# Where a second product stands between first products: moving TensorE's work to the last step of each batch

## The chip, the cores and the metric

The kernel runs on one core of a Trainium2 chip. The metric is the device time of one execution in microseconds. The core has five engines with a queue each: TensorE (PE, matrix products), VectorE (DVE), ScalarE (ACT), GpSimd (POOL) and SyncE (SP, which issues the transfers). TensorE writes its products into eight PSUM banks of 128 x 512 float32, from which ScalarE and VectorE read them.

## The reference, cut to what matters

```python
def _attn_ref(x, state):                 # x (4, 8, 512, 64), state (4, 8, 32, 64)
    a = softmax(scale * x @ state.T)     # xread = a @ state
    a2 = softmax(scale * state @ x.T)    # sread = a2 @ x
    return concat([xread, sread])        # 4 batches of 512 + 32 tokens, 512 wide

def _moe_ref(x, w_in, w_out):            # w_in (512, 2048), w_out (2048, 512)
    h = x @ w_in
    g = np.maximum(h, 0.0) + np.log1p(np.exp(-np.abs(h)))
    return (g @ w_out)

def _moe2_ref(x, w_gate, w_val, w_out):  # 512 -> 1536 -> 512
    g = x @ w_gate
    silu = g * (1.0 / (1.0 + np.exp(-g)))
    return (silu * (x @ w_val) @ w_out)
```

The three run one after the other: attention, then the layer with the softplus, then the layer with the gate.

## The kernel before

Every float32 operand of the two layers is split in two float32r parts, a high one (a copy, on ScalarE, which rounds) and a low one (whole minus high, `low`, L77, on VectorE or GpSimd). A product is then three matmuls, high x high, low x high and high x low (`mm3`, L71 to 74), each of 128 x 128 by 128 x 512.

**Prologue.** It loads tokens and states, does the softmaxes and the states' reads, and makes the first weights. **Stage 1** is the layer with the softplus, the loop of L800 to L825. **Stage 2**, the loop of L880 to L932, is the gated layer.

Stage 1 works on units (c, b, ft): chunk c of four takes 512 of the 2048 hidden columns, b is one of four batches of 512 tokens, and ft one of four tiles of 128 hidden columns. There are 64 units and 64 steps n. A unit is a first product `p1` (L419; six matmuls into a bank `ph`), a softplus on ScalarE twice (`h` rounded and `C` whole, L411 and L414), a subtraction on GpSimd (`l`, `g_low`, L433) and a second product `p2` (L442; twelve matmuls into four banks `py`, one for each 128 output columns, which collect over the four ft of a batch). After ft 3 the four `py` are added to the sums `yacc` by VectorE (`y_add`, L451; in the first chunk L456 copies, in the others L458 adds), two at the start of the step's VectorE work and two later. The second products of the next batch start in the same four banks, so they wait for these. In step n TensorE does `p2` of unit n, then what hangs on the step, then `p1` of unit n + LAG, with LAG = 4 (L806 to L808); ScalarE and GpSimd then make `h`, `C` and `l` of unit n + 3.

What hangs on a step is put there by `at(step, kind, function)`: "pe" runs between `p2` and `p1`; "dve0" at the start of VectorE's work of the step (ahead of the first `y_add`), "dve1" at its end; "act" and "pool" likewise. On TensorE three things hang there in every chunk but the last, for the chunk that comes next: eight products `pm` of three matmuls (`m_mm`, L369), which give the tokens' factors `m` from the weights `win` (copied by ScalarE, L396, and subtracted by VectorE, `m_low`, one step later); and the state tokens' own layer, `s1` (L507; twelve matmuls into `ps`), a softplus, `s2` (four transposes into `ptgs`), a copy and a subtraction for the result `gs`, `s3` (L532; twelve matmuls into `ps`) and `s4` (L540; VectorE, the sum into `ys`, L545). VectorE also prepares weights (`t_win`, `t_wo`, `t_gv`, `t_w`; L122 to L140), for the next chunk and, in the last chunks, for stage 2, and in the last chunk sums of `yacc` that stage 2 reads (`y_sums`, L474 to L480, results `T`).

TensorE's, VectorE's and SyncE's orders are as the code writes them. ScalarE's and GpSimd's are set by a scheduler. An allocator gives each product a PSUM bank: four tags, 4 banks for "y", 3 for "h" (`ph`) and 1 for "m" (`pm`, `ps`, `ptgs`), share eight banks, and which product gets which bank, and so for whose eviction it has to wait, changes with the order. In chunk c, steps count from 16 c.

Of the kernel before, what the change touches and what calls it, by code (L numbers as in the profile page):

```python
# [22 lines left out]
def attention_moe_moe2_kernel(  # L23
# [44 lines left out]
    def bank(tag, name):  # L68
        return psum.tile([P, 512], F32, tag=tag, bufs=BUFS[tag], name=name)

    def mm3(o, a, b, first, last, **k):  # L71

        for i, (s, t) in enumerate(((0, 0), (1, 0), (0, 1))):
            nc.tensor.matmul(o, a[s], b[t], start=first and i == 0, stop=last and i == 2, **k)  # L74
# [344 lines left out]
    def p1(u):  # L419
        c, b, ft = u  # L420
        ps = bank("h", f"ph{c}_{b}_{ft}")
        f = slice(ft * P, (ft + 1) * P)
        for hg in range(NHG):
            mm3(
                ps, [mt[c, b, hg][:, i, f] for i in range(2)], [aT[b, hg][:, i, :] for i in range(2)],
                hg == 0, hg == NHG - 1,
            )
        n = f"{c}_{b}_{ft}"
        sp[u] = Softplus(
            ps, work.tile([P, 512], F32, tag="C", name=f"C{n}"), work.tile([P, 512], F32R, tag="GH", name=f"h{n}")  # L430
        )

    def g_low(u):  # L433
        l = work.tile([P, 512], F32R, tag="GL", name="l%d_%d_%d" % u)
        low(nc.gpsimd, l, sp[u].g, sp[u].h)
        gT[u] = (sp[u].h, l)
# [5 lines left out]
    def p2(u):  # L442
        c, b, ft = u
        if ft == 0:
            for dt in range(KT):
                yps[dt] = bank("y", f"py{c}_{b}_{dt}")
        t = gT.pop(u)
        for dt in range(KT):
            mm3(yps[dt], [wo[c, ft].out[:, i, dt * P:(dt + 1) * P] for i in range(2)], t, ft == 0, ft == FT - 1)

    def y_add(c, b, dt):  # L451
        if c == 0 and dt % 2 == 0:
            yacc[b, dt // 2] = slot([P, 2, 512], F32, "yacc", f"yacc{b}_{dt // 2}")
        v = yacc[b, dt // 2][:, dt % 2, :]
        if c == 0:
            nc.vector.tensor_copy(v, yps[dt])  # L456
        else:
            nc.vector.tensor_tensor(out=v, in0=yps[dt], in1=v, op=ALU.add)  # L458
# [118 lines left out]
    act = {}  # L577
# [79 lines left out]
    LAG = 4  # L657
    M_STEPS = (6, 7, 9, 10, 14, 15, 17, 18)
    with tc.manual_schedule(engines={ENG.PE}):
        units = [(c, b, ft) for c in range(NCK) for b in range(B) for ft in range(FT)]  # L660
        NU = len(units)
# [45 lines left out]
        def at(n, kind, fn, *args):  # L707
            hooks.setdefault((n, kind), []).append((fn, args))

        def run(n, kind):  # L710
            for fn, args in hooks.get((n, kind), ()):
                fn(*args)

        def at_weights(n, late, store, key, make):

            def begin():
                store[key] = make(*key)
            at(max(0, n - 4), "load", begin)
            for m, kind, step in (
                (n, "dve0", "head"), (n, "act", "square"), (n + late, "dve1", "tail"),  # L720
                (n + late + 1, "act", "high"), (n + late + 1, "pool", "low"),
            ):
                at(m, kind, lambda step=step: getattr(store[key], step)())

        for c in range(NCK):
            n0 = c * UC
            if c + 1 < NCK:
                pieces = [(win, piece_win, (c + 1, k)) for k in range(KT)] + [(wo, piece_wo, (c + 1, k)) for k in range(FT)]
            else:
                pieces = []  # L730
            for i, (store, make, key) in enumerate(pieces):
                n, late = n0 + i // 2 * FT + i % 2, 2 - 2 * (i % 2)
                at_weights(n, late, store, key, make)
            if c + 1 < NCK:
                for i in range(2 * KT):
                    n = n0 + M_STEPS[i]
                    k = (c + 1, i // KT, i % KT ^ 1)
                    at(n, "pe", m_mm, *k)
                    at(n, "act", m_high, *k)
                    at(n + 1, "dve0", m_low, *k)  # L740
            if c + 1 < NCK:
                for i, kind, fn in (
                    (10, "pe", s1), (11, "act", s1_first), (16, "pe", s2), (16, "act", s2_high), (17, "dve0", s2_low),
                    (20, "pe", s3), (21, "dve0", s4),
                ):
                    at(n0 + i, kind, fn, c + 1)
        for k in range(1, KT):
# [52 lines left out]
        with tc.manual_schedule(engines={ENG.DVE, ENG.SP}):  # L800
            for n in range(1 - LAG, NU):
                run(n, "load")
                if n >= 0:
                    u = units[n]
                    p2(u)
                    run(n, "pe")  # L806
                    if n + LAG < NU:
                        p1(units[n + LAG])  # L808
                nx = units[n + LAG - 1] if n + LAG - 1 < NU else None
                if nx:  # L810
                    sp[nx].high()
                    sp[nx].whole()
                last = n >= 0 and u[2] == FT - 1
                run(n, "dve0")
                for dt in range(2) if last else ():
                    y_add(u[0], u[1], dt)
                run(n, "act")
                if nx:
                    g_low(nx)
                run(n, "pool")  # L820
                for dt in range(2, KT) if last else ():
                    y_add(u[0], u[1], dt)
                run(n, "dve1")
                run(n, "act1")
                run(n, "pool1")  # L825
            for n in range(NU, NU + FT + 1):
                for kind in ("act", "dve0", "pool"):
                    run(n, kind)
# [11 lines left out]
        for k, j in enumerate(range(len(EARLY), 3 * NF)):  # L840
            n, half = divmod(k, 2)
# [134 lines left out]
```

## Time and profile before

| what | us |
|---|---|
| median of 3 runs | 788.11 (787.13 to 790.48) |
| the profiled execution | 788.33 |
| its span | 786.4 |
| TensorE busy | 743.8 (95%) |
| VectorE busy | 511.2 (65%) |
| ScalarE busy | 354.1 (45%) |
| GpSimd busy | 418.7 (53%) |

What ends last is followed back through TensorE for 69% of the span, and through VectorE for 15%. The shares are an average over stages: stage 1 has the waits, stage 2 hardly any. Matmuls overlap at their ends, so 389 ns of busy time for one go with starts 227 ns apart.

### The profile page before, as it was taken

How to read it: one execution, taken by the hardware profiler on the slowest of the kernel's cores; microseconds unless marked ns; L12 is line 12 of the kernel's file. 1: busy time of each engine (PE TensorE's matmuls, PEld its weight loads, DVE VectorE, ACT ScalarE, POOL GpSimd, SP SyncE). 2: the span in 40 equal slices, each digit the busy share in tenths (PEclk: the TensorE clock that was granted, in tenths of full speed). 3: DMA queues.
4: the chain of work that ended last, by engine and by line, in shares of the span. 5: the costliest groups of instructions: out<-in, count | busy, mean ns of one | idle time of the engine just before them, and what ended most of it. 6: DMA issues, size and time to landing. Idle time of an engine off the chain costs nothing.

```text
span 786.4 us, 9643 instructions
## 1 busy us (share of the span) xinstructions
PE 743.8 (95%) x3280; PEld 600.9 (76%) x3280; DVE 511.2 (65%) x725; ACT 354.1 (45%) x643; POOL 418.7 (53%) x371
## 2 busy tenths in 40 slices
PE   6586999999999999899899999999999999999997
PEld 3345787888788888777678888888888888888886
DVE  5899586686887688779668767575563343343334
ACT  5576465464656555654354444433253223322320
POOL 3578465547565747688467667655355213212311
PEclk9688999999999999999899999999999999999999
DMA  9712132424343424455739798978437737436412
GB/s 340 298 57 80 54 135 82 133 81 145 109 142 114 162 79 152 143 193 200 276 126 349 271 379 313 314 276 325 161 119 273 230 141 248 155 133 231 158 40 108
DMA packets 51217, 144.03 MB, mean 183 GB/s; under 512 B 5728, under 2 KB 18016, under 8 KB 51168
## 3 DMA queue, kind: packets, MB, share of 16 engines
q1 hardware_dynamic: 51168, 143.42, 52.3%
q8 instruction: 26, 0.43, 0.2%
q14 instruction: 23, 0.19, 0.1%
HBM read 107.48 MB, written 35.91 MB: 182 GB/s over the span
## 4 chain that ended last, share of the span: by engine, by line
PE 69%; DVE 15%; DMA 6%; issue 4%; POOL 4%; ACT 2%; SPq 1%; DVEq 0%; ACTq 0%; POOLq 0%
PE py L74 18%; PE po L74 15%; PE px L74 14%; PE pz L74 7%; PE ph L74 6%; PE pt L74 3%; DMA gw<-gv_d 2%; DMA raw_gv<-in_moe_w_val_dram 2%; PE ps L74 2%; PE pm L74 2%; DVE m L77 1%; POOL l L77 1%; DVE t_wo L136 1%; DVE yacc L458 1%; DVE t_gv L126 1%
## 5 line engine op out<-in xcount | busy, mean ns | idle before, releaser
L74 PE MATMUL py<-h,wo 128*128 128x512 f32 x512 | 162.7, 400 | 9.8 <-DVE yacc L458 8.0
L74 PE MATMUL po<-w,h 128*128 128x512 f32 x384 | 126.2, 391 | 0.0
L74 PEld LDWEIGHTS py<-h,wo 128*128 128x128 f32 x512 | 98.3, 193 | 32.4 <-DVE yacc L458 9.8
L77 POOL TENSOR_TENSOR l<-C,h 128x512 fp32r<-128x512 f32 x64 | 90.5, 1416 | 44.9 <-ACT C L414 40.6
L77 POOL TENSOR_TENSOR l<-cA,h 128x512 fp32r<-128x512 f32 x24 | 35.2, 1465 | 143.9 <-ACT h L582 143.9
L74 PE MATMUL py<-l,wo 128*128 128x512 f32 x256 | 102.1, 399 | 5.0 <-POOL l L77 5.0
L74 PE MATMUL ph<-aT,m 128*128 128x512 f32 x384 | 97.8, 391 | 1.4 <-DVE m L77 1.1
L603 DVE TENSOR_TENSOR oacc<-po,oacc 128x512 f32<-128x512 f32 x80 | 54.7, 690 | 56.5 <-PE po L74 56.2
L74 PEld LDWEIGHTS ph<-aT,m 128*128 128x128 f32 x384 | 71.9, 188 | 16.8 <-issue 1.3
L74 PEld LDWEIGHTS po<-w,h 128*128 128x128 f32 x384 | 72.1, 188 | 14.8
L74 PE MATMUL po<-w,l 128*128 128x512 f32 x192 | 74.8, 390 | 0.5 <-POOL l L77 0.5
L77 DVE TENSOR_TENSOR m<-pm,m 64x512 fp32r<-64x512 f32 (+1 forms) x60 | 41.2, 687 | 45.3 <-ACT m L396 41.2
L74 PE MATMUL px<-T_0s,gw 128*128 128x512 f32 x216 | 61.3, 392 | 1.8 <-ACT cC L907 1.7
L74 PEld LDWEIGHTS py<-l,wo 128*128 128x128 f32 x256 | 49.4, 193 | 16.1 <-POOL l L77 5.4
L74 PE MATMUL px<-T_1s,gw 128*128 128x512 f32 x216 | 60.7, 389 | 0.0
L191 POOL TENSOR_TENSOR sums_gv<-t_gv 128x128 f32<-128x128 f32 x48 | 23.0, 500 | 53.2 <-DVE t_gv L140 49.8
L896 DVE TENSOR_TENSOR cA<-py,cA 128x512 f32<-128x512 f32 x24 | 16.5, 689 | 50.2 <-PE py L74 46.9
L74 PEld LDWEIGHTS px<-T_0s,gw 128*128 128x128 f32 x216 | 40.1, 188 | 11.6 <-ACT cC L907 2.6
L582 ACT ACTIVATE h<-cA 128x512 fp32r<-128x512 f32 x24 | 15.2, 632 | 71.6 <-DVE cA L915 71.6
L74 PEld LDWEIGHTS px<-T_1s,gw 128*128 128x128 f32 x216 | 40.5, 188 | 8.5
L74 PEld LDWEIGHTS po<-w,l 128*128 128x128 f32 x192 | 36.1, 188 | 8.3 <-POOL l L77 1.0
L77 POOL TENSOR_TENSOR l<-cC,h 128x512 fp32r<-128x512 f32 x24 | 31.8, 1326 | 18.8 <-ACT h L582 17.3
(159 smaller groups left out, 1517.5 us busy)
## 6 DMA issues: line engine op xcount, KB each, us to landing
gw<-gv_d SPq DMA_DIRECT2D x96, 512.0 KB, 6.6
gv_d<-gv SPq DMA_DIRECT2D x24, 512.0 KB, 3.3
gv_d<-split_gv SPq DMA_DIRECT2D x24, 512.0 KB, 4.0
w<-w_d SPq DMA_DIRECT2D x24, 512.0 KB, 8.8
raw_win<-in_moe_w_in_dram SPq DMA_DIRECT2D x16, 512.0 KB, 4.6
raw_wo<-in_moe_w_out_dram SPq DMA_DIRECT2D x16, 512.0 KB, 3.8
raw_gv<-in_moe_w_gate_dram SPq DMA_DIRECT2D x48, 128.0 KB, 3.3
raw_gv<-in_moe_w_val_dram SPq DMA_DIRECT2D x48, 128.0 KB, 2.8
```

What stands on the lines that cost most here:

```text
L74: nc.tensor.matmul(o, a[s], b[t], start=first and i == 0, stop=last and i == 2, **k)
L77: eng.tensor_tensor(out=o, in0=whole, in1=high.bitcast(F32), op=ALU.subtract)
L126: nc.vector.scalar_tensor_tensor(out=ti, in0=self.top, scalar=-0x40000000, in1=ti, op0=ALU.bitwise_and, op1=ALU.bitwise_or,)
L136: nc.vector.scalar_tensor_tensor(out=ti, in0=self.bot, scalar=29, in1=ti, op0=ALU.logical_shift_right, op1=ALU.bitwise_or,)
L191: nc.gpsimd.tensor_tensor(out=o, in0=x, in1=y, op=op)
L458: nc.vector.tensor_tensor(out=v, in0=yps[dt], in1=v, op=ALU.add)
L582: nc.scalar.activation(h, src, AF.Copy)
L603: nc.vector.tensor_tensor(out=v, in0=ps, in1=v, op=ALU.add)
L896: nc.vector.tensor_tensor(out=c["A"], in0=y, in1=c["A"], op=ALU.add)
```

## The change

Two edits. In the loop, `p1` is no longer called once a step for unit n + 4: in the steps of ft 0 and 1 it still is, in that of ft 2 none is called, and in that of ft 3 two are, for units n + 3 and n + 4. In the table, three steps of the state tokens move: `s1` from the third step of a batch (10) to the fourth (11), `s3` from the first step of a batch (20) to the last of the one ahead of it (19), and `s4` from VectorE's start of step 21 to its end of step 20.

```diff
                 for i, kind, fn in (
-                    (10, "pe", s1), (11, "act", s1_first), (16, "pe", s2), (16, "act", s2_high), (17, "dve0", s2_low),
-                    (20, "pe", s3), (21, "dve0", s4),
+                    (11, "pe", s1), (11, "act", s1_first), (16, "pe", s2), (16, "act", s2_high), (17, "dve0", s2_low),
+                    (19, "pe", s3), (20, "dve1", s4),
                 ):
...
                     p2(u)
                     run(n, "pe")
-                    if n + LAG < NU:
-                        p1(units[n + LAG])
+
+
+                    for k in ((n,), (n,), (), (n - 1, n))[u[2]]:
+                        if k + LAG < NU:
+                            p1(units[k + LAG])
```

In the changed file, lines below the loop are three further down. VectorE's queue has the same order as before from the start of stage 1 on. The other engines' orders follow here at three places; names carry the batch and the tile (the chunk is left out), then a number.

TensorE at the boundary of steps 51 and 52 in the last chunk, before: the end of the first step of batch 1, whose `py` are done before `ps` (`s3`).

```order
L74 MATMUL ph_1_3_3007<-aT_1_250,m_1_1_2557 128x512 x3
L74 MATMUL py_1_0_3046<-h_1_0_2877,wo_0_2653 128x512 x2
...
L74 MATMUL py_1_3_3049<-l_1_0_2936,wo_0_2653 128x512
L74 MATMUL ps_3062<-wo_0_2653,gs_2885 128x512 x3
L74 MATMUL ps_3062<-wo_1_2614,gs_2885 128x512 x3
L74 MATMUL ps_3062<-wo_2_2827,gs_2885 128x512 x3
L74 MATMUL ps_3062<-wo_3_2782,gs_2885 128x512 x3
L74 MATMUL ph_2_0_3075<-aT_0_305,m_2_0_2784 128x512 x3
```

And now, from the last `py` of batch 0 on:

```order
L74 MATMUL py_0_3_2851<-l_0_3_2892,wo_3_2773 128x512
L74 MATMUL ps_2998<-wo_0_2653,gs_2885 128x512 x3
L74 MATMUL ps_2998<-wo_1_2591,gs_2885 128x512 x3
L74 MATMUL ps_2998<-wo_2_2827,gs_2885 128x512 x3
L74 MATMUL ps_2998<-wo_3_2773,gs_2885 128x512 x3
L74 MATMUL ph_1_2_3011<-aT_0_201,m_1_0_2422 128x512 x3
L74 MATMUL ph_1_2_3011<-aT_1_250,m_1_1_2557 128x512 x3
L74 MATMUL ph_1_3_3020<-aT_0_201,m_1_0_2422 128x512 x3
L74 MATMUL ph_1_3_3020<-aT_1_250,m_1_1_2557 128x512 x3
L74 MATMUL py_1_0_3059<-h_1_0_2877,wo_0_2653 128x512 x2
```

Between the last `py` of batch 0 and the first of batch 1 stood six matmuls (one `ph`); now 24 stand there (`ps` and two `ph`). In the other batches it is twelve.

ScalarE in the second chunk around steps 21 to 23, before (`m` is the copy of a `pm` into the two batches' factors, `split_gv` that of sums which GpSimd makes):

```order
L411 ACTIVATE h_2_1_1666<-ph_2_1_1658 128x512
L414 ACTIVATE C_2_1_1665<-ph_2_1_1658 128x512
L396 ACTIVATE m_0_0_1713<-pm_0_1_1693 64x512
L396 ACTIVATE m_1_0_1715<-pm_0_1_1693 64x512
L195 ACTIVATE split_gv_1_1809<-sums_gv_1_1767 128x512
L411 ACTIVATE h_2_2_1705<-ph_2_2_1697 128x512
```

And now:

```order
L411 ACTIVATE h_2_1_1667<-ph_2_1_1659 128x512
L414 ACTIVATE C_2_1_1666<-ph_2_1_1659 128x512
L195 ACTIVATE split_gv_1_1809<-sums_gv_1_1767 128x512
L396 ACTIVATE m_0_0_1704<-pm_0_1_1693 64x512
L396 ACTIVATE m_1_0_1706<-pm_0_1_1693 64x512
L396 ACTIVATE m_0_0_1704<-pm_0_0_1728 64x512
L396 ACTIVATE m_1_0_1706<-pm_0_0_1728 64x512
L411 ACTIVATE h_2_2_1740<-ph_2_2_1732 128x512
```

The copy of `pm_0_1` stood ahead of `split_gv` and now stands behind it. In the banks, `ph_2_2` here is in the bank that `pm_0_1` had; before, the two had different ones. Other such pairs in the changed program, each a product in the bank of the one named behind it: in step 7 `ph` of batch 2, ft 2 and the `pm` of the same step; in step 11 `ps` and the `ptgs` of step 10; in step 47 `ph` of batch 0, ft 2 and the `pm` of step 46.

GpSimd in the last chunk, from the sums of batch 0 to the first `l` of batch 3, before:

```order
L77 TENSOR_TENSOR l_2_2_3214<-C_2_2_3152,h_2_2_3153 128x512
L191 TENSOR_TENSOR sums_gv_1_3220<-t_gv_1_3156,sums_gv_1_3220 128x128
L77 TENSOR_TENSOR B_0_0s<-yacc_1_1031,B_0_0s 128x512
L77 TENSOR_TENSOR l_2_3_3267<-C_2_3_3197,h_2_3_3198 128x512
L77 TENSOR_TENSOR split_gv_1_3260<-sums_gv_1_3220,split_gv_1_3260 128x512
L77 TENSOR_TENSOR B_0_1s<-yacc_1_1031,B_0_1s 128x512
L77 TENSOR_TENSOR l_3_0_3298<-C_3_0_3250,h_3_0_3251 128x512
L77 TENSOR_TENSOR w_3374<-t_w_3254,w_3374 128x512
```

And now:

```order
L77 TENSOR_TENSOR l_2_1_3156<-C_2_1_3118,h_2_1_3119 128x512
L77 TENSOR_TENSOR B_0_0s<-yacc_1_1031,B_0_0s 128x512
L77 TENSOR_TENSOR l_2_2_3214<-C_2_2_3188,h_2_2_3189 128x512
L77 TENSOR_TENSOR split_gv_1_3260<-sums_gv_1_3220,split_gv_1_3260 128x512
L77 TENSOR_TENSOR B_0_1s<-yacc_1_1031,B_0_1s 128x512
L77 TENSOR_TENSOR l_2_3_3267<-C_2_3_3197,h_2_3_3198 128x512
L77 TENSOR_TENSOR w_3374<-t_w_3254,w_3374 128x512
L77 TENSOR_TENSOR l_3_0_3298<-C_3_0_3250,h_3_0_3251 128x512
```

Each `l` has moved behind work for stage 2 that stood after it.

## Rows read from the trace of the kernel before

**Rows 1.** Windows, stages 1 and 2: busy us (instructions) by engine, clock, DMA share, GB/s.

```profile
67.00:391.00 324.00, 306.95 (x1327) 251.06 (x1326) 249.36 (x323) 170.60 (x305) 201.43 (x176) 0.97 0.41 137
391.00:786.40 395.40, 388.65 (x1778) 322.06 (x1776) 207.43 (x294) 139.93 (x242) 177.85 (x160) 1.00 0.61 216
```

**Rows 2.** Waits of TensorE: total us, times, longest us.

```profile
PE py L74 <- DVE yacc L458: 8.0, 2, 5.3
PE py L74 <- POOL l L77: 5.0, 1, 5.0
```

**Rows 3.** Timeline of TensorE: start us, us, operation, count, [idle before and its releaser].

```profile
132.78 1.62 PE L74 MATMUL ph<-aT,m 128*128 128x512 f32 x6 [1.12 <-DVE m L77]
211.07 2.74 PE L74 MATMUL ps<-win,sT 128*128 128x512 f32 x11 [1.13 <-DVE m L77]
334.94 1.22 PE L74 MATMUL py<-h,wo 128*128 128x512 f32 x2 [2.68 <-DVE yacc L458]
363.79 0.62 PE L74 MATMUL py<-h,wo 128*128 128x512 f32 x2
367.87 0.62 PE L74 MATMUL py<-h,wo 128*128 128x512 f32 x2
377.42 1.22 PE L74 MATMUL py<-h,wo 128*128 128x512 f32 x2 [5.31 <-DVE yacc L458]
```

**Rows 4.** Windows over three second products and over VectorE's stretch without a wait.

```profile
343.29:346.17 2.88, 2.88 (x14) 2.41 (x13) 2.78 (x5) 1.91 (x4) 0.21 (x1) 1.00 0.94 349
334.94:339.37 4.43, 4.43 (x13) 3.59 (x14) 2.90 (x5) 4.34 (x8) 4.43 (x6) 0.65 0.42 169
377.42:382.73 5.31, 5.31 (x14) 4.15 (x15) 2.89 (x4) 3.56 (x8) 4.73 (x5) 0.53 1.00 334
...
342.12:376.69 34.57, 29.99 (x132) 24.32 (x130) 34.12 (x35) 15.62 (x28) 27.07 (x23) 0.98 0.63 215
```

**Rows 5.** Timeline of VectorE, as rows 3.

```profile
114.57 1.38 DVE L77 TENSOR_TENSOR m<-pm,m 64x512 fp32r<-64x512 f32 x2
194.90 1.39 DVE L77 TENSOR_TENSOR m<-pm,m 64x512 fp32r<-64x512 f32 x2 [2.89 <-ACT m L396]
334.19 2.49 DVE L458 TENSOR_TENSOR yacc<-py,yacc 128x512 f32<-128x512 f32 x4
337.05 0.83 DVE L126 SCALAR_TENSOR_TENSOR t_w<-raw_w,t_w 128x512 int32<-128x512 int32 x1
342.12 0.69 DVE L545 TENSOR_TENSOR ys<-ps,ys 128x512 f32<-128x512 f32 x1 [4.25 <-PE ps L74]
343.80 0.68 DVE L77 TENSOR_TENSOR B_0s<-yacc,B_0s 128x512 fp32r<-128x512 f32 x1
364.84 1.78 DVE L476 TENSOR_TENSOR yacc<-yacc,yacc 128x512 f32<-128x512 f32 x1
376.69 2.47 DVE L458 TENSOR_TENSOR yacc<-py,yacc 128x512 f32<-128x512 f32 x4
```

**Rows 6.** Waits of VectorE over the span, as rows 2.

```profile
DVE ys L545 <- PE ps L74: 9.8, 3, 4.3
```

**Rows 7.** Timeline of GpSimd, as rows 3.

```profile
340.24 1.29 POOL L77 TENSOR_TENSOR l<-C,h 128x512 fp32r<-128x512 f32 x1
345.96 1.45 POOL L191 TENSOR_TENSOR sums_gv<-t_gv 128x128 f32<-128x128 f32 x2 [3.18 <-DVE t_gv L140]
364.33 1.75 POOL L77 TENSOR_TENSOR l<-C,h 128x512 fp32r<-128x512 f32 x1
368.42 1.29 POOL L77 TENSOR_TENSOR B_1s<-yacc,B_1s 128x512 fp32r<-128x512 f32 x1 [0.64 <-ACT B_1s L490]
374.62 1.59 POOL L77 TENSOR_TENSOR w<-t_w,w 128x512 fp32r<-128x512 f32 x1 [3.22 <-ACT w L146]
```

**Rows 8.** Timeline of ScalarE, as rows 3.

```profile
193.67 1.20 ACT L396 ACTIVATE m<-pm 64x512 fp32r<-64x512 f32 x2
197.37 0.63 ACT L195 ACTIVATE split_gv<-sums_gv 128x512 fp32r<-128x512 f32 x1 [2.50 <-POOL sums_gv L191]
```

## The prediction

> **What bounds the kernel now.** I read the windows by stage first, then the waits of TensorE, then the moments of those waits, then VectorE and GpSimd in the last chunk. Stage 2 (391 to 786.4 us) is bound by TensorE: busy 388.65 of 395.40 us at granted clock 1.00 [rows 1]. Nothing in it is edited and its instructions on VectorE keep their order, so I carry it unchanged; whatever stage 1 ends earlier or later, the program does. Stage 1 holds TensorE busy for 306.95 of 324.00 us [rows 1], so 17 us is all that any reordering could win, plus what the clock costs. The waits name most of it: 8.0 us for `y_add` on VectorE in two waits and 5.0 once for the first `l` [rows 2]. The two are at 334.94 (2.68 us) and 377.42 (5.31 us); two smaller ones, 1.12 at 132.78 and 1.13 at 211.07, are for an `m` of VectorE whose bank a `ph` and a `ps` take over [rows 3]. Behind the two long ones TensorE starts at its lower clock level: granted 0.65 over the second product that follows at 334.94 and 0.53 over that at 377.42, against 1.00 over one that follows no wait, at 343.29 [rows 4]. Twelve matmuls and their tail take 2.88 us there, 4.43 at 0.65 and 5.31 at 0.53, so the clock adds 1.55 and 2.43 us to the waits of 2.68 and 5.31.
>
> The two long waits have different causes. At 334.94 VectorE is in time with its queue, and the six matmuls of one `ph` between the two batches (1.36 us at the pace of 0.227 us a matmul, which is 2.72 us for the twelve of a second product; 363.79 to 367.87 is one of each [rows 3]) are too short a cover for the four `y_add` (2.49 us from 334.19 [rows 5]). At 377.42 VectorE itself is late. It waits 4.25 us for `ps`, starts `ys` at 342.12 [rows 5], and has hardly a gap from there on: 34.12 us busy in the 34.57 us up to the `y_add` of 376.69 [rows 4]. So this last boundary is set by when VectorE begins at 342.12 and how fast it then works. Its speed hangs on GpSimd. An operation of two SBUF inputs takes 1.78 us at 364.84 beside a GpSimd operation of 1.75 us at 364.33, while one of the same size takes 0.68 us at 343.80, where GpSimd pauses until 345.96; GpSimd's `l` takes 1.29 us at 340.24, in the stretch where VectorE waits [rows 5, 7]. While both run, one of each takes about 1.75 us, against 0.68 + 1.29 = 1.97 one after the other: running together saves 11%, no more.
>
> **The change, part by part.** No instruction is added or removed in the stage, so at full clock TensorE's own work is unchanged; SyncE's transfers change neither number nor size, and VectorE's queue keeps its order through the stage (the end of step 20 is the place ahead of the start of step 21, so `s4` passes nothing there). What moves is TensorE's order, and with it the scheduler's orders of ScalarE and GpSimd and the PSUM banks.
>
> (1) *Two `ph` and, once a chunk, `s3` between two batches.* Two `ph` take 12 x 0.227 = 2.72 us, with `s3` 5.44, against 1.36. At 334.94 the cover grows by 4.08 us and the loss there is 2.68 + 1.55 = 4.23, so that stall nearly goes; it is the largest sure gain on TensorE. By itself it does not enter the sum: VectorE sets the next boundary, and what TensorE gains here it waits for at 377.42. At the other boundaries there was no wait to win.
>
> (2) *VectorE no longer waits for `ps`.* Without a lag `s3` now ends at 332.1, some 10 us earlier: the `ph` of steps 50 and 51, the `py` of step 52 and the lost 4.23 us no longer stand before it. VectorE was free at 337.88, so `ys` could start up to 4.25 us earlier; waits of the same sort in two chunks before make the sum 9.8 us over three [rows 6], off the critical path. But in those 4.25 us GpSimd ran alone at 1.29 us [rows 7]; now both run together. By the 11% above, 4.25 us of GpSimd and some 4 us of VectorE that now run together are worth 0.11 x 8.3 = 0.9 us, against 4.25 if VectorE kept its pace of 0.69. I take 0.5, since the lag of TensorE, below, delays the `y_add` of that boundary as well. The Trainium skill (SBUF — State Buffer, Who interferes with whom) says that a VectorE instruction with two SBUF inputs contends with a GpSimd instruction that reads SBUF, and that the one that comes second is blocked until the first has finished. The rows above go the same way (1.78 beside 1.75), though some 1.75 for a pair is less than the sum of both; by the strict rule the earlier start would be worth 0 instead of 0.5.
>
> (3) *New owners of PSUM banks.* The allocator now gives some `ph` the bank of an `m` product that is evicted later. In step 7 `ph` of batch 2, ft 2 takes the bank of the `pm` of that step, whose `m` subtraction stands in VectorE's queue behind the `y_add` and runs at 114.57 to 115.95 [rows 5]; TensorE would be there at 113.4, so it waits 2.6 us. In step 11 `ps` takes the bank of the transposed tokens, which are copied (0.6) and subtracted (0.69) only behind what stands ahead of them: some 2, estimated, with the 1.12 of step 10 gone. Step 23 is the dearest: `ph` takes the bank of the `pm` of step 22, whose `m` was copied by ScalarE at 193.67 and subtracted by VectorE at 194.90; in ScalarE's new order that copy stands behind `split_gv`, which waited until 197.37 for GpSimd's sums [rows 5, 8]. Copy 1.2 and subtraction 1.4 after that give 200.6, two `ph` 203.3, and the next second product started at 197.54: 5.8 later, with the `y_add` of that step queued behind. Step 47 repeats it with nothing to wait for from GpSimd: some 1.6, the two subtractions of an `m` and what is queued before them. The bounds of all four are 0 (if the sums come earlier) and their sum, 12. Against them go 1.13 of 211.07 [rows 3] and some quarter microseconds. I carry a lag of TensorE of +3 after step 12, +6 after 24 and +5.5 at step 48. It is paid out of the stall that (1) removes (4.23) and out of the 5.31 us of waiting at 377.42: TensorE had that much to spare.
>
> (4) *Later `l` in the last chunk.* GpSimd's new order puts every `l` behind one or two more operations: that of the last step of batch 2 ran at 364.33, 1.8 us before its second product at 367.87; it now stands behind B_1s (368.42) and would end near 371.4, a wait of some 3 us on TensorE [rows 3, 7]. This too lies inside the wait that ended at 377.42. The `l` of the first step of the last batch now stands behind `w` (374.62 and 1.59 long [rows 7]), so it ends near 377.9: +0.6 on the path.
>
> (5) *The clock at the last boundary.* By (3) and (4) TensorE reaches the last boundary late and in pieces, so that its idle stretch there is some 1 to 2 us instead of 5.31. After the wait of 1.12 us six matmuls took 1.62 us [rows 3], 0.1 over six starts and a tail at full clock. Then the 2.43 us of 377.42 are won. Bounds: 0 and 2.43; I take 2.43.
>
> (6) *The prologue* has another order on ScalarE and GpSimd; the first `l` stands behind two more subtractions of 1.29 us, which would make the 5.0 us wait [rows 2] longer by up to 2.6, while what those subtractions delayed before comes earlier: -1.5 to +1.5, taken as 0.
>
> Sum against the profiled execution: 788.33 - 0.5 (2) - 2.43 (5) + 0.6 (4) = 786.0. The median of the runs is 788.11, 0.2 below that execution, so I leave 786.0.
>
> **The rivals.** *The gain is kept in full* (0.25): the sums of step 22 come in time, the lag is under 3 us, VectorE starts `ys` 4.25 us earlier and works off its short operations before GpSimd takes the port; then the last `y_add` is 3 to 4.25 us earlier and the clock gains 2.43: 788.3 - 4.25 - 2.43 = 781.6, or 783 with part of it. For it: in 342 to 346 VectorE did have GpSimd's pause. Against: it now has GpSimd's three operations there.
> *Slower* (0.17): the bank waits of (3) and GpSimd's order of (4) are not absorbed. It decides when TensorE's lag at step 48 passes what `ys` can spare: `s3` would end at 332.1 plus the lag, and VectorE is free at 337.88, so from a lag of 5.8 on VectorE starts later by the rest, and from 5.8 + 4.25 = 10 on it starts later than now. With all four waits at their price (12) and nothing won back before step 48 but 2.3, the lag is near 10, and late `l` on GpSimd add 3 + 2.6 that then are on the path: +4 to +8, about 793.
> *Nothing moves* (0.13): VectorE and GpSimd in sum set the last boundary, TensorE waits long enough there to lose its clock as now, and the gain at 334.94 is only waited for later: 788 to 789.
> *The forecast* (0.45) lies at 784.5 to 787.5.
>
> **How the numbers follow.** Half a per cent is 3.9 us, about what a measurement of this kernel can tell from no change. Faster by more: the full gain, 0.25, and the lower end of the forecast, 0.04. Slower by more: 0.17. Within: the rest, 0.54. The range goes from the full gain (781.5) to the near end of the slower case (792): it leaves out the very best tail and about two thirds of the slower one.
>
> **What would show it.** Right: no wait at the boundary of steps 51 and 52; no wait of VectorE for `ps`; clock 1.00 in the first second product of the last batch; new waits of `ph` for `m` in steps 7 and 23, of 2 to 6 us each; operations of VectorE at 1.7 us where `ys` now stands; stage 2 at 395 us. Wrong: clock 0.5 in the last batch (then 788 or more), the last `y_add` more than 2 us earlier (then 783), TensorE over 10 us late at step 48, or a stage 2 that differs by more than 1 us.

## The result and the profile after

The changed kernel takes 799.78 us (median of 4 runs, 798.28 to 801.45) against 788.33 (4 runs, 787.13 to 790.48): a ratio of 1.0143, interval 1.0113 to 1.0173. It is slower by three times what a measurement can tell, and above the whole range. The profiled execution took 799.57 us, so 13.6 us stand between it and the forecast.

The page gives the busy times, and a window the second stage (busy us and instructions of TensorE, its weight loads, VectorE, ScalarE and GpSimd; then TensorE's clock, DMA share, GB/s).

```profile
span 797.8 us, 9665 instructions
PE 745.7 (93%) x3280; PEld 603.2 (76%) x3280; DVE 509.0 (64%) x725; ACT 354.7 (44%) x643; POOL 417.3 (52%) x371
```

```profile
401.40:797.80 396.40, 388.74 (x1777) 323.27 (x1775) 203.97 (x294) 140.43 (x242) 176.37 (x160) 1.00 0.62 217
```

All engines do the work they did before. Stage 2 begins at 401.4 and not at 391.3 and takes 396.4 us instead of 395.1 (the row of [rows 1] begins a little earlier, at 391.00): ten of the eleven microseconds are lost in stage 1. There the two waits for `y_add` of [rows 2] have gone from the list of TensorE's waits, and these stand in it (total us, times, longest):

```profile
PE ph L74 <- DVE m L77: 7.2, 3, 5.1
PE py L74 <- POOL l L77: 4.0, 2, 2.0
...
PE px L74 <- ACT cC L910: 3.1, 2, 2.4
...
PE ps L74 <- DVE yacc L456: 2.4, 1, 2.4
...
PE ps L74 <- DVE gs L77: 1.8, 1, 1.8
```

TensorE's timeline has the moment of each (start, us, operation, count, idle time before and its releaser):

```profile
113.91 4.62 PE L74 MATMUL ps<-win,sT 128*128 128x512 f32 x12 [2.41 <-DVE yacc L456]
...
138.55 3.06 PE L74 MATMUL ps<-win,sT 128*128 128x512 f32 x12 [1.81 <-DVE gs L77]
...
206.31 4.81 PE L74 MATMUL ph<-aT,m 128*128 128x512 f32 x12 [5.12 <-DVE m L77]
...
286.47 3.00 PE L74 MATMUL ph<-aT,m 128*128 128x512 f32 x12 [1.22 <-DVE m L77]
...
325.72 2.96 PE L74 MATMUL ph<-aT,m 128*128 128x512 f32 x12 [0.89 <-DVE m L77]
...
362.90 0.50 PE L74 MATMUL py<-l,wo 128*128 128x512 f32 x1 [2.01 <-POOL l L77]
...
383.16 0.50 PE L74 MATMUL py<-l,wo 128*128 128x512 f32 x1 [2.00 <-POOL l L77]
...
389.91 0.61 PE L74 MATMUL py<-h,wo 128*128 128x512 f32 x2
...
424.11 0.96 PE L74 MATMUL px<-T_0s,gw 128*128 128x512 f32 x3 [2.44 <-ACT cC L910]
```

The first five are products whose PSUM bank another product still holds. Two of them cost more than the wait itself. Windows over the twelve matmuls behind these two show it; the third window is the first second product of the last batch, which follows no wait:

```profile
113.91:118.53 4.62, 4.62 (x13) 3.65 (x14) 4.47 (x7) 1.96 (x4) 2.26 (x2) 0.63 0.03 7
206.31:211.12 4.81, 4.81 (x13) 3.87 (x14) 4.73 (x9) 1.64 (x3) 0.65 (x1) 0.60 0.01 3
389.91:392.80 2.89, 2.89 (x15) 2.37 (x14) 0.95 (x2) 1.54 (x4) 2.89 (x3) 1.00 1.01 339
```

At a granted clock of 0.63 and 0.60 twelve matmuls take 4.62 and 4.81 us, against 2.88 at 1.00 [rows 4]: 1.74 and 1.93 us behind waits of 2.41 and 5.12.

How late TensorE is can be read where each second product starts. The differences to before, in us (the last two columns are experiments below; at step 52 all three kernels have already done the 2.72 us of `s3`, which before came after that start):

| second product of step | before, start | after | `s1` at 10 | two banks |
|---|---|---|---|---|
| 4 | 93.57 | +2.8 | -0.3 | +2.6 |
| 8 | 116.10 | +5.0 | -0.3 | +0.5 |
| 12 | 138.34 | +5.8 | -1.6 | -0.8 |
| 24 | 197.54 | +13.4 | -1.9 | -1.1 |
| 40 | 275.87 | +13.4 | -1.8 | -1.9 |
| 48 | 313.94 | +14.6 | -1.5 | -1.2 |
| 52 | 334.94 | +14.5 | -1.4 | -1.1 |
| 60 | 377.42 | +12.5 | -2.2 | -1.2 |
| end of stage 1 | 391.35 | +10.1 | -4.6 | -3.6 |

The 14.6 us at step 48 are made of few things: 0.7 left of the prologue's +2.8, step 7 with 2.41 + 1.74, step 11 with 1.81 + 0.2 - 1.12 (the old wait of [rows 3] is gone), step 23 with 5.12 + 1.93 + 0.1, step 26 with the other old wait gone (-1.3), and steps 39 and 47 with 1.3 and 1.0. They sum to 13.9. From there to the end of stage 1 the gains that the prediction named do come: the stall at 52 (4.2) and the wait and clock at 60 (5.31 + 2.43). But the two waits for `l` cost 4.0, and 3.5 more in the matmuls behind them (22 starts from 383.16 to 389.91 take 6.75 us at a granted clock of 0.75, against 4.99 at the pace of 0.227; behind the other wait they take 6.76): 14.6 - 4.2 - 7.7 + 7.5 = 10.2, against 10.1 measured. Stage 2 adds 1.3, with a wait of 2.44 for `cC` at 424.11 (the longest such wait before was 1.0).

VectorE's timeline in the last chunk shows what became of the earlier `ys`:

```profile
346.62 2.48 DVE L458 TENSOR_TENSOR yacc<-py,yacc 128x512 f32<-128x512 f32 x4
...
350.23 0.68 DVE L545 TENSOR_TENSOR ys<-ps,ys 128x512 f32<-128x512 f32 x1
...
351.89 1.79 DVE L77 TENSOR_TENSOR B_0s<-yacc,B_0s 128x512 fp32r<-128x512 f32 x1
...
372.61 1.78 DVE L474 TENSOR_TENSOR T<-yacc,yacc 128x512 f32<-128x512 f32 x1
...
387.80 2.47 DVE L458 TENSOR_TENSOR yacc<-py,yacc 128x512 f32<-128x512 f32 x4
```

`ys` no longer waits (no bracket; [rows 5] has 4.25 us there), yet it runs 8.1 us later than before, because the `y_add` ahead of it came 12.4 later. `B_0s`, behind it, takes 1.79 us where it took 0.68 in GpSimd's pause before. From that `y_add` to the next VectorE needs 387.80 - 346.62 = 41.2 us instead of 42.5 [rows 5].

### The profile page after: what moved, and what is told of

The parts are those of the page before. It is cut to its first block, busy times and chain, and to the rows that moved or that the text cites. A ratio compares the mean times of both kernels' runs of the same rounds, so it can differ in the third digit from the quotient of the medians.

```text
span 797.8 us, 9665 instructions
## 1 busy us (share of the span) xinstructions
PE 745.7 (93%) x3280; PEld 603.2 (76%) x3280; DVE 509.0 (64%) x725; ACT 354.7 (44%) x643; POOL 417.3 (52%) x371
## 4 chain that ended last, share of the span: by engine, by line
PE 52%; DVE 6%; POOL 5%; issue 4%; ACT 3%; DMA 0%; DVEq 0%; ACTq 0%; POOLq 0%
PE po L74 16%; PE px L74 15%; PE py L74 8%; PE pz L74 7%; PE pt L74 3%; PE ph L74 2%; POOL l L77 2%; DVE m L77 1%; DVE yacc L458 1%; POOL sums_gv L191 1%; POOL split_gv L77 1%; ACT m L396 1%; POOL gv L77 1%; DVE t_win L136 1%; ACT h L411 0%
## 5 line engine op out<-in xcount | busy, mean ns | idle before, releaser
L74 PE MATMUL py<-h,wo 128*128 128x512 f32 x512 | 159.6, 393 | 0.0
L74 PE MATMUL ph<-aT,m 128*128 128x512 f32 x384 | 99.9, 405 | 7.2 <-DVE m L77 7.2
L74 PEld LDWEIGHTS ph<-aT,m 128*128 128x128 f32 x384 | 74.9, 197 | 24.9 <-issue 7.8
L77 DVE TENSOR_TENSOR m<-pm,m 64x512 fp32r<-64x512 f32 (+1 forms) x60 | 41.2, 686 | 61.7 <-ACT m L396 55.9
L74 PEld LDWEIGHTS px<-T_1s,gw 128*128 128x128 f32 x216 | 40.6, 188 | 8.5
L411 ACT ACTIVATE h<-ph 128x512 fp32r<-128x512 f32 x64 | 37.6, 588 | 10.3 <-PE ph L74 10.1
L910 ACT ACTIVATE cC<-px 128x512 f32<-128x512 f32 x24 | 14.3, 598 | 61.7 <-PE px L74 61.7
```

What stands on the lines that cost most here:

```text
L77: eng.tensor_tensor(out=o, in0=whole, in1=high.bitcast(F32), op=ALU.subtract)
L411: nc.scalar.activation(self.h, self.ps, AF.Softplus)
L910: nc.scalar.activation(c["C"], x, AF.Copy)
```

## The experiments

**Theories.** *A*: the new owners of PSUM banks (steps 7, 11, 23, 39, 47), which come with `s1` one step later and its other prologue, make TensorE late, and that lag is the loss. *B*: two first products in one step, with `l` made later, cost it. *C*, put only before the second four runs: `s1` beside two first products in step 11 costs by itself, whoever holds the banks. Ratios are to the kernel before in the same series, with their intervals; its medians were 789.43 in the first four runs, 789.35 in the next four, 789.8 in the last two. The diffs start from the changed kernel unless the text says otherwise.

### The states' first product back in its old step

```diff
-                    (11, "pe", s1), (11, "act", s1_first), (16, "pe", s2), ...
+                    (10, "pe", s1), (11, "act", s1_first), (16, "pe", s2), ...
```

> The changed kernel with one number put back: `s1` at step 10, all else as changed. In the built order VectorE's whole queue is then as before, the prologue too, and no `ph` of ft 2 stands in the bank of a `pm`. Theory A (new bank owners and the new prologue, both brought in by `s1` at step 11, cost the time): no wait of TensorE for `m` in step 23, lag at step 48 near 0, total 783 to 788 us. Theory B (the two `ph` in one step, with their later `l` on GpSimd, cost the time): 795 to 800 us, with waits for `l` in steps 55 and 59 as in the changed kernel.

Measured: 786.33 us, 0.9972 (0.9956 to 0.9988). One digit in the table takes the whole loss away, with both `ph` still in one step. TensorE's waits in this kernel, and the first second product of the last batch:

```profile
PE py L74 <- POOL l L77: 9.3, 5, 4.9
...
PE py L74 <- DVE yacc L456: 1.8, 1, 1.8
...
PE ps L74 <- DVE m L77: 1.4, 1, 1.4
PE py L74 <- DVE yacc L458: 1.2, 2, 1.0
```

```profile
368.57 0.79 PE L74 MATMUL py<-l,wo 128*128 128x512 f32 x1 [2.33 <-POOL l L77]
```

```profile
375.25:378.14 2.89, 2.89 (x15) 2.37 (x14) 1.04 (x2) 1.48 (x4) 2.89 (x3) 1.00 0.95 333
```

No `ph` waits for an `m`; one wait of 1.4 for a bank is left. The late `l` are all there (2.33 us at 368.57; the 4.9 is the old wait in step 0) and the kernel still comes out 0.3% under the one before, less than the half per cent that I trust but surely no loss: against B. The clock in the last batch is 1.00.

### The later first product alone

The kernel before with only `s1` moved (`p1` each step, `s3` and `s4` in their old steps).

```diff
-                    (10, "pe", s1), (11, "act", s1_first), (16, "pe", s2), ...
+                    (11, "pe", s1), (11, "act", s1_first), (16, "pe", s2), ...
```

> The kernel before with one number changed: `s1` at step 11 instead of 10; `p1` every step and `s3` at 20 as before. Its prologue order is that of the changed kernel, and `ps` of step 7 takes the bank of a `py`; the pair of step 23 (`ph` behind `pm`) isn't there. Theory A: slower by the waits of steps 7 to 11 with their clock, 4 to 6 us, part of it absorbed later: 790 to 794. Theory B: 787 to 789, no different from before.

Measured: 786.96 us, 0.9965 (0.9949 to 0.998). It is not slower, against A as I had put it: the move by itself even takes both old bank waits away (1.12 and 1.13 of [rows 3]; 0.18 is left). On C it says nothing, since only one first product stands in step 11 here.

```profile
112.55 3.01 PE L74 MATMUL ps<-win,sT 128*128 128x512 f32 x12 [0.69 <-DVE yacc L456]
...
333.81 0.73 PE L74 MATMUL py<-h,wo 128*128 128x512 f32 x2 [2.13 <-DVE yacc L458]
...
376.39 1.22 PE L74 MATMUL py<-h,wo 128*128 128x512 f32 x2 [5.20 <-DVE yacc L458]
```

The stalls for `y_add` stay (2.13 and 5.20). The pair of step 7 is there, with 0.69. So the loss needs `s1` in step 11 together with another part of the change.

### The states' second product alone

The kernel before with only `s3` and `s4` moved.

```diff
-                    (20, "pe", s3), (21, "dve0", s4),
+                    (19, "pe", s3), (20, "dve1", s4),
```

> The kernel before with `s3` at step 19 and `s4` at the end of step 20 alone. Prologue and VectorE's queue as before. Theory A: TensorE's wait at 334.94 (2.68 us) and VectorE's for `ps` (4.25 us) go; VectorE then works beside GpSimd, so its last `y_add` comes 0 to 1.5 us earlier: 784.5 to 788. If the full 4.25 us are kept: 781 to 784. Theory B says nothing of it beyond 788.

Measured: 789.05 us, 0.9994 (0.9976 to 1.0012): no change, where I had expected 784.5 to 788. Its trace is of an execution of 792.14 us, 3.1 above that median. The boundary of steps 51 and 52 does lose its wait, but an earlier one gains a wait that before had none:

```profile
202.18 0.73 PE L74 MATMUL py<-h,wo 128*128 128x512 f32 x2 [2.29 <-DVE yacc L458]
...
381.22 1.22 PE L74 MATMUL py<-h,wo 128*128 128x512 f32 x2 [3.66 <-DVE yacc L458]
```

### The states' second product back in its old step

```diff
-                    (19, "pe", s3), (20, "dve1", s4),
+                    (20, "pe", s3), (21, "dve0", s4),
```

> The changed kernel with `s3` and `s4` put back (20, 21), `s1` at 11 and two `ph` in the last step kept. Prologue as changed, steps 7 and 11 with the same bank owners as changed, but in step 23 `ph` stands behind `ps` of step 20, not behind `pm`. Theory A: the 5.1 us wait of step 23 and the 1.8 us of clock behind it go, and the wait for `ps` on VectorE returns off the path: 791 to 795. Theory B: 798 to 801.

Measured: 805.74 us, 1.0205 (1.0178 to 1.0233), some 5 us slower still: 16.3 above the kernel before of its series, where the changed kernel is 11.5 above. It lies above both ranges. I had expected the dear wait of step 23 to go. It passed to another pair of products, the `pm` of step 23 behind that of step 22, and step 39 became dearer:

```profile
115.44 4.61 PE L74 MATMUL ps<-win,sT 128*128 128x512 f32 x12 [2.39 <-DVE yacc L456]
...
205.88 1.62 PE L74 MATMUL pm<-win,bdr 128*128 128x512 f32 x3 [4.05 <-DVE m L77]
...
289.26 4.57 PE L74 MATMUL ph<-aT,m 128*128 128x512 f32 x12 [2.84 <-DVE m L77]
```

TensorE is 19.2 us late at step 48. Each order of the code makes its own pairs.

### A second bank for the products of the factors

The only edit is the number of banks that `pm`, `ps` and `ptgs` may hold at a time. TensorE's order is word for word that of the changed kernel; VectorE's is the same from 82 us on (step 1). What differs is who follows whom in a bank, the prologue, and what the scheduler makes of ScalarE's and GpSimd's orders.

```diff
-    BUFS = {"y": 4, "h": 3, "m": 1}
+    BUFS = {"y": 4, "h": 3, "m": 2}
```

> The changed kernel with two banks instead of one under the tag of `pm`, `ps` and `ptgs` (`BUFS`, 4, 3, 2). TensorE's order is that of the changed kernel, instruction for instruction; the bank owners are new ones: no `ps` behind a `py` in step 7, no `ph` of ft 2 behind a `pm` in steps 7, 23, 39 or 47; VectorE's, ScalarE's and GpSimd's orders differ a little from the prologue on. Theory A (who owned the bank before costs the time, and the clock behind each wait): the lag of TensorE at step 48 is within 3 us of zero and the time 784 to 788 us. Theory C (`s1` next to two `ph` in step 11 costs by itself, whatever the banks): 796 to 800.

Measured: 784.39 us, 0.9939 (0.9918 to 0.996); the same kernel in the last series:

> The two-bank kernel again, in the same series, to be set against the hand-ordered one: 783.5 to 785.5 us, 0.994 of the kernel before.

785.04 us, 0.9938 (0.9916 to 0.996). With TensorE's order unchanged, all bank waits over 1 us in stage 1 are gone and with them some 16 us (from 11.5 above the kernel before to 5.0 below). This is the closest test, and it is for A and against C, which had 796 to 800: TensorE's order is not at fault, the owners of the banks are, with what the scheduler makes of them on ScalarE (the copy of `m` ahead of step 24 is in time here, below). At step 23 the run doesn't part the two, the bank's owner and ScalarE's order. Both engines' rows at the last boundaries read as the prediction wanted them, VectorE first:

```profile
336.55 0.68 DVE L545 TENSOR_TENSOR ys<-ps,ys 128x512 f32<-128x512 f32 x1
...
339.18 1.78 DVE L77 TENSOR_TENSOR B_0s<-yacc,B_0s 128x512 fp32r<-128x512 f32 x1
```

```profile
369.54 0.50 PE L74 MATMUL py<-l,wo 128*128 128x512 f32 x1 [2.10 <-POOL l L77]
...
376.27 0.62 PE L74 MATMUL py<-h,wo 128*128 128x512 f32 x2
```

`ys` without a wait, 5.6 us earlier than in [rows 5]; operations of two SBUF inputs at 1.78 right behind it; no wait at 376.27. The kernel before with two such banks wasn't tried, so what the second bank alone would give stays open.

### Two first products in a step from the second chunk on

```diff
-                    for k in ((n,), (n,), (), (n - 1, n))[u[2]]:
+                    for k in ((n,), (n,), (), (n - 1, n))[u[2]] if u[0] else (n,):
```

> The changed kernel with one `p1` a step in the first chunk and the changed rule from the second on. Prologue as changed; steps 7 and 11 have the bank owners of the kernel with `s1` at 11 alone (a wait of some 0.7 us there), steps 23, 39 and 47 the pairs `ph` behind `pm` of the changed one. Theory A: the 4.3 us of step 7 with its clock and the 0.8 of step 11 go, the 7.2 of step 23 stay: lag at step 48 of 8 to 10 us, 793 to 796. Theory C: 787 to 789, since step 11 of the first chunk is single again, or 799 if all chunks count.

Measured: 795.26 us, 1.0074 (1.0046 to 1.0101), as A had it (793 to 796) and outside what C had (787 to 789, or 799). Step 7 waits 0.67 instead of 2.41 and step 23 keeps its wait:

```profile
113.90 3.04 PE L74 MATMUL ps<-win,sT 128*128 128x512 f32 x12 [0.67 <-DVE yacc L456]
...
200.24 4.58 PE L74 MATMUL ph<-aT,m 128*128 128x512 f32 x12 [4.79 <-DVE m L77]
```

TensorE's lag at step 48 is 8.6 instead of 14.6, and the time some 5 us less (5.9 above the kernel before instead of 11.5): the first chunk's waits cost that much, and the rest is there without them.

### Two first products in the last chunk only, and none

First the edit with the condition of the last chunk, then the kernel before with the three table entries alone (`p1` each step).

```diff
-                    for k in ((n,), (n,), (), (n - 1, n))[u[2]]:
+                    for k in ((n,), (n,), (), (n - 1, n))[u[2]] if u[0] == NCK - 1 else (n,):
```

> The changed kernel with the changed rule for `p1` in the last chunk only, `s1`, `s3` and `s4` as changed. No pair `ph` of ft 2 behind a `pm` that is evicted later. Theory A: TensorE goes as in the kernel with `s1` at 11 alone up to step 48, then no wait at the boundary of steps 51 and 52 and none of VectorE for `ps`; 783.5 to 787. Theory C: 787 to 790.

> The kernel before with the three moved steps of the table alone (`s1` 11, `s3` 19, `s4` end of 20), `p1` once a step throughout. Theory A: 784 to 788; VectorE has no wait for `ps`, the last `y_add` is 0 to 1.5 us earlier than with `s1` alone. Theory C: 787 to 790.

Measured: 790.17 us, 1.0012 (0.9997 to 1.0028), and 789.34, 1.0001 (0.9985 to 1.0018). I expected a gain from both, since neither has a bank wait in step 23; both missed A's range and came out near or in C's, 787 to 790. That doesn't speak for C, since neither has two first products in step 11. The wait is another one. VectorE's row of the second kernel for the last factor ahead of the boundary of steps 23 and 24, and TensorE's behind it:

```profile
197.08 1.39 DVE L77 TENSOR_TENSOR m<-pm,m 64x512 fp32r<-64x512 f32 x2 [7.26 <-ACT m L396]
```

```profile
199.12 1.22 PE L74 MATMUL py<-h,wo 128*128 128x512 f32 x2 [2.31 <-DVE yacc L458]
...
377.99 1.22 PE L74 MATMUL py<-h,wo 128*128 128x512 f32 x2 [4.35 <-DVE yacc L458]
```

VectorE waits 7.26 us for a copy that ScalarE makes only behind `split_gv` (2.89 before, [rows 5]; 7.25 with the early `s3` alone, 7.21 in the changed kernel; 3.04 with `s1` at 10, 3.05 with two banks). The `y_add` behind it is late, and one `ph` doesn't cover it: 2.31 us, in a place that had no wait (2.29 in the first of the two kernels). So the early `s3` gained nothing in the three kernels that have one `ph` at step 23, while the kernel with `s1` at 10 and the one with two banks have the paired `ph` too, and gain. That the pair covers the late copy is not shown: in those two the copy is in time, and the changed kernel and the one with two `ph` from the second chunk on, where it is late, have the bank pair of step 23 as well.

### GpSimd's order written out in the last chunk

The two-bank kernel, with GpSimd's order as written from step 50 on, and `l` ahead of what else hangs on the step.

```diff
+                with tc.manual_schedule(engines={ENG.Pool}) if n >= NU - UC + 2 else ExitStack():
...
+                    if nx:
+                        g_low(nx)
                     run(n, "act")
-                    if nx:
-                        g_low(nx)
```

Two theories on what is left: *A1*, the late `l` bound the last chunk; *A2*, VectorE does, beside GpSimd.

> The kernel with two banks for `pm` (the one before this) with GpSimd's order written by hand in the last 14 steps: each `l` ahead of the splitting of weights of its step. TensorE's order is the same. The two-bank kernel waited 5.6 us for `l` in steps 53 to 59. Theory A1 (those waits are on the path at the last boundary): they fall under 2 us, the last `y_add` is 1 to 2.5 us earlier: 1 to 3 us under the two-bank kernel, 781.5 to 783.5. Theory A2 (VectorE beside GpSimd sets the last boundary whatever comes first): within 1 us of the two-bank kernel, 783.5 to 785.5.

Measured: 784.43 us, 0.9938 (0.9918 to 0.9959), the same as the two-bank kernel of its series. The waits of TensorE over 1 us in its last chunk:

```profile
342.34 0.50 PE L74 MATMUL py<-l,wo 128*128 128x512 f32 x1 [1.43 <-POOL l L77]
...
350.72 0.73 PE L74 MATMUL py<-h,wo 128*128 128x512 f32 x2 [3.10 <-DVE yacc L458]
...
371.39 1.19 PE L74 MATMUL py<-h,wo 128*128 128x512 f32 x2 [3.72 <-ACT T_1s L490]
```

The waits for `l` in the last chunk fall to one of 1.43. TensorE reaches step 48 at 307.45 instead of 312.07, 4.6 us ahead (it waits 1.31 for the first `l` instead of 9.30), and ends stage 1 only 1.6 ahead; it waits 3.10 for a `y_add` and 3.72 at the next boundary, where the profile names a copy on ScalarE that ended just behind that boundary's first `y_add`. VectorE needs 42.0 us between the two `y_add`, against 41.25 in the two-bank kernel. That is for A2: with the lag gone, VectorE's stretch sets the end, and a TensorE that is ahead waits.

## Why the prediction was wrong

**Step (3), the banks, is the step that failed, in the size of the lag: 14.6 us at step 48 instead of 5.5.** The sum held nothing for the lag, because 5.5 was to be paid by the stalls of 4.23 and 5.31 at the two boundaries; 14.6 was not. It is also one of the prediction's own signs of being wrong (over 10 us late at step 48). The pairs that the prediction named show in three steps: step 23 with a wait of 5.12, step 11 with 1.81 (2 forecast), step 47 with 0.89 (1.6). The 5.8 that it had for step 23 was no wait but how late the next second product would start against before; that became 13.4. Of the 9.1 us that were missing:

- *3.7 are the clock behind the new waits*, 1.74 and 1.93. The prediction priced exactly that behind the old waits, and gave the new ones none.
- *2.1 are waits of a chain that were not added up.* I took the time at which `m` of step 22 is ready (200.6) as fixed and let half of the lag of step 12 vanish in it, so that step 23 added 3. In the changed kernel `split_gv` itself starts 5.5 us later than in [rows 8], since GpSimd's sums stand in a queue with work that hangs on TensorE: the `l` ahead of them starts at 193.88 instead of 188.32, 5.6 later. ScalarE's rows, then VectorE's:

```profile
202.89 0.63 ACT L195 ACTIVATE split_gv<-sums_gv 128x512 fp32r<-128x512 f32 x1 [2.71 <-POOL sums_gv L191]
203.55 2.28 ACT L396 ACTIVATE m<-pm 64x512 fp32r<-64x512 f32 x4
```

```profile
204.77 1.39 DVE L77 TENSOR_TENSOR m<-pm,m 64x512 fp32r<-64x512 f32 x2 [7.21 <-ACT m L396]
206.09 2.47 DVE L458 TENSOR_TENSOR yacc<-py,yacc 128x512 f32<-128x512 f32 x4
```

  These are the steps that the prediction named, in its order, with the end of `m` at 206.16 and not 200.6. The lag of 6 stayed and the 5.12 came on top.
- *The rest is small*: 0.7 from the prologue, 1.7 between steps 26 and 48, where a fifth pair (1.22 in step 39) took back what the old wait of [rows 3] gave, 0.3 in step 7, and some 0.6 in small gaps between steps 12 and 24 that I can't put down to one thing. In step 7 I overlooked a pair (`ps` in the bank of a `py` that VectorE copies late). The named one, `ph` behind `pm`, shows no wait there; that 2.41 came out so near the 2.6 put on it is luck.

**Steps (1) and (5) hold**: no wait at 51 to 52, clock 1.00 over the first second product of the last batch. Their 4.2 and 7.7 us (5.31 of wait and 2.43 of clock) did come and went into the lag, but the lag was larger than both together.

**Step (2) holds in kind, and its size was too small.** VectorE loses its wait for `ps`, runs beside GpSimd at 1.78, and does its stretch in 41.2 instead of 42.5 us: 1.3 us where I took 0.5 and bounded by 4.25. The other kernels with the early `s3` need 40.6 to 42.0, those with the old one (the later `s1` alone, and `s3` back) 42.6 and 42.9. By the strict rule of the Trainium skill (SBUF — State Buffer, Who interferes with whom), in which the second of the two is blocked until the first has finished, it would be 0; the rows lie nearer to it than to 4.25.

**Step (4)** had later `l`, and one of the two places: step 59 waits 2.00 where 3 was forecast. The +0.6 of the sum, at the first step of the last batch, didn't show: `l` makes no wait there. Step 55, with 2.01, was not forecast. What the waits cost depends on (3): with the lag 7.5 us with their clock; without it, as in the kernel with `s1` at 10 and the one with two banks, TensorE waits for `l` too (2.33 at 368.57, 2.10 at 369.54) and still ends stage 1 earlier than before.

**Step (6)** was +0.7 for 0. **Stage 2** was to stay the same and took 1.3 us more. From its first matmul it takes 396.4 to 397.8 us in the profiles with two `ph` and 394.3 to 395.6 in the four without; two profiles of the same two-bank kernel differ by 1.2 (396.6 and 397.8). The wait of 2.3 to 2.6 for `cC` is in all of them but three (the kernel before, the later `s1` alone, the early `s3` alone, with 1.0), so it doesn't go by the two `ph`. Its cause was not tested.

The sum closes: the forecast had stage 1 end 2.3 us earlier than before; it ended 10.1 later; that and 1.3 make 13.7 of the 13.6 us. The rival *slower* had the right mechanism and the right point: a lag of over 10 at step 48 decides. Its price was too low (+4 to +8 for +11.2), since its lag stopped near 10, and its chance too, since I held the four waits at their full price for a bound and not for the likely value. Where the lag is taken away, the time lies near the forecast of 786.0: 786.3 with `s1` in its old step, 784.4 and 785.0 with a second bank, the best version here, 0.6% under the kernel before. That is in part luck and doesn't prove the sum: stage 1 ends 4.6 and 3.6 us earlier there and not 2.3, stage 2 takes 1.3 to 2.5 longer, and the later `s1` alone comes to 786.96 with both old stalls in place.

## What to carry to other kernels

When an order changes under an allocator, list for each product who held its bank, and follow that owner's eviction to the engine and what stands ahead of it there; waits of one dependent chain add up, each with the clock's loss behind it, until some engine is shown to have slack at that place. A later wait pays a lag only up to its own size; compare the two before a gain at the end is booked. When a reordering that should gain loses, hold the order and change the number of buffers: here that one edit took some 16 us off, with TensorE's order the same.

## What the runs showed of the hardware

The loss of clock behind a wait doesn't follow the length of the wait in these rows: 1.74 us behind 2.41 and 1.93 behind 5.12 (granted clock 0.63 and 0.60 over twelve matmuls), 1.8 behind the 2.0 for `l` (0.75 over 22 starts), but 0.2 and 0.1 behind 1.81 and 1.22 (twelve matmuls in 3.06 and 3.00 us, granted 1.00). In the kernel before it was 1.55 behind 2.68 and 2.43 behind 5.31 [rows 4]. The wait of 2.01 in step 55 and that of 1.81 in step 11 differ by a tenth in length, their cost by 1.6 us. What TensorE did just before them differs too, so the length alone need not be the reason; it wasn't tried apart.
